# An attention, expert and FFN kernel: first expert chosen from two batches, five attention buffers, rows in sorted order

## The chip, the cores and the metric

One core of one Trainium2 chip runs the whole kernel. The metric is device time in microseconds (us) of one execution. The engines are named as in the profile: PE (TensorE matmul), PEld (its weight loads), DVE (VectorE), ACT (ScalarE), POOL (GpSimd) and SP (SyncE, which here only issues transfers).

## The reference

Three stages follow each other. Shapes: batch 4, 8 heads, 768 positions, head size 64, so 3072 tokens of 512 numbers.

```python
# 1. chunked attention: 24 chunks of 32 queries, each with 16 positions to the left,
#    8 to the right, and 8 memory keys
scores = scale * q_c @ k_full.T; a = softmax(scores); out[:, :, c] = a @ v_full
# 2. top-1 mixture of 8 experts on x = (tokens, 512)
logits = xn @ en.T / tau                 # xn, en: rows divided by their norms
expert_idx = argmax(logits); gate_w = softmax(logits)[expert_idx]
out[mask_e] = gate_w * (relu(x[mask_e] @ w1[e]) @ w2[e])      # w1 512x1024, w2 1024x512
# 3. FFN
h = x @ w_in; g = relu(h) ** 2; y = g @ w_out                 # 512 -> 2048 -> 512
```

## The kernel before, in words

**Attention** runs over 32 iterations i (4 batches, 4 pairs of heads, 2 halves of the sequence), as a software pipeline over the engines with five more iterations to empty it. In iteration i PE does, in this order, `sp` (scores of i, L277, 24 matmuls in two groups of 12), `op` (values of i-2, L336), `lp` (router products, L382), `tp` (transposes of the weights of i-1, L324) and `xp` (transposes of the output of i-3, L371). DVE does a small `memset` into `sp`, `rs` (row sums, L311), in every second iteration the inverse of the sums (L317, L318), `mx` (L293), `e` (scores minus maxima, L301) and `xa` (output scaled, L350). ACT copies `tp` to `pt`, takes exponents of `e`, copies `xp` to `xt` and takes squares of rows for the norms. POOL lays the windows of keys into `kw` for iteration i+2 (two copies L135 and one of the memory keys L267). SP loads q, k and v (`qt`, `kt`, `vb`, 384 KB each and v twice that per pair of iterations). Before the change q, k and v have three buffers each.

When the four pairs of heads of a half batch are through, `dp` and a copy give its `dots` (the router logits, 3 tiles of 128 tokens), and the rows go to `x_d` in DRAM.

**Early choice.** The generator `early` is stepped between the parts of the last attention iterations. It counts over finished tiles which expert is most frequent (`cs`, `cm`, `sel`, `ks`, then the number `e_i`, which SP and POOL read as a register in order to start loading the weights of that expert, `r1a`, `r1b`), ranks the tokens of that expert over 18 of the 24 tiles (three batches; `m0`, `p0`, `g0`, `osl`, `lf`, then a comparison with a row of numbers into `scratch`, `rid`, `ip`, `iv`), and gathers 2 slots of 128 of its rows from `x_d`. So the first expert can start before the routing of all the rest is known. The weights are split into a high and a low part in fp32r: a cast on ACT (`wh1a`, `wh1b`) and a subtraction on DVE (`wl1a`, `wl1b`); the split of `r1a` is step W0, that of `r1b` W1. Steps are listed in a string, by the (iteration minus 32) in which they stand: x0, x1 transpose the gathered rows, A0 begins the first product (`hps`).

**Routing.** After the last `dots`, `stp` (PE, counts per expert) starts a chain of small DVE operations (`ce`, `key`, `ahead`, `tri_c`, `byp`, `pm`, `dlr`, `pos`, `osl`, `rid`, `ohl`), which gives each token its slot (31 slots of 128). The experts of the other slots and then the FFN follow; from there on PE is nearly always busy.

Of the kernel before, what the change touches and what calls it, by code (L numbers as in the profile page):

```python
# [9 lines left out]
F32 = mybir.dt.float32  # L10
# [11 lines left out]
def kernel(  # L22
# [70 lines left out]
    ks = route.tile([P, 1], F32, name="ks")  # L93
    e0 = route.tile([P, 1], F32, name="e0")
# [5 lines left out]
    sumb = route.tile([P, 2, 2, E], BF16, name="sumb")  # L100
# [118 lines left out]
    def attention(actx, hooks, space, drain):  # L219
# [6 lines left out]
        q_p = qk_ctx.enter_context(tc.tile_pool(name="qt", bufs=3))  # L226
# [5 lines left out]
        NV, NW, NK_, LAG = 3, 3, 3, 2  # L232
# [189 lines left out]
        nc.scalar.copy(out=vb[1][:, 0].rearrange("p c d -> p (c d)"), in_=kt[0][:, 0:1].to_broadcast([P, 2 * NC * D]))  # L422
# [6 lines left out]
        clear_kw(0, nc.vector)  # L429
        clear_v(1, 1, nc.vector)  # L430
# [5 lines left out]
        clear_kw(1, nc.vector)  # L436
        windows(1)
        def start_en():
# [3 lines left out]
            vec.extend([lambda: next(gen, None)] * 17)  # L442
# [6 lines left out]
        def finish_en():  # L449
# [7 lines left out]
            0: [lambda: clear_v(2, 0, nc.gpsimd), start_en, lambda: clear_kw(2, nc.vector)],  # L457
            1: [lambda: clear_v(2, 1, nc.gpsimd)],
# [3 lines left out]
        load_q(1)  # L462
        load_k(2)
# [18 lines left out]
        for i in range(NK + LAG + 3):  # L482
            if i == NK:
                qk_ctx.close()
                space()
# [82 lines left out]
    def tally(c, pool, part):  # L568
# [3 lines left out]
        lt = pool.tile([P, E, n], F32, name=f"lt{part}", tag=f"lt{part}")  # L572
        sums = pool.tile([P, 2, E, 1], F32, name=f"sums{part}")
        revb = c["rev"].unsqueeze(1).to_broadcast([P, n, E])
        kmb = km[:, T0:T1].to_broadcast([P, n, E])
        nc.vector.tensor_tensor(out=o, in0=revb, in1=kmb, op=ALU.is_equal)
        yield
        nc.vector.tensor_tensor(out=lt.rearrange("p e t -> p t e"), in0=kmb, in1=revb, op=ALU.is_gt)
        yield
        nc.vector.tensor_reduce(out=sums[:, 1], in_=o.rearrange("p t e -> p e t"), op=ALU.add, axis=AX.X)  # L580
        yield
        nc.vector.tensor_reduce(out=sums[:, 0], in_=lt, op=ALU.add, axis=AX.X)
        yield
        nc.vector.tensor_copy(out=sumb[:, part], in_=sums.rearrange("p j e o -> p j (e o)"))
        yield

    def early(c, per, ps, begin, gather):
# [9 lines left out]
        G = 2 * HT  # L597
        kme = km[:, 0:TE].rearrange("p t o -> p (t o)")
        pe = p0g[:, 0:TE].rearrange("p t o -> p (t o)")
        nc.vector.memset(p0g[:, TE:NT], 0.0)  # L600
        o0 = t([P, TE, E], BF16, "o0")
        for T0 in range(0, TE, G):
# [6 lines left out]
            yield int(T0 + G < TE)  # L609
        yield from gap((6, 1, 6, 1, 8, 6)[0])  # L610
        cp = ps.tile([P, G, E], F32, name="cp", tag="a")
        for T0 in range(0, TE, G):
            nc.tensor.matmul(out=cp, lhsT=c["ones"], rhs=o0[:, T0:T0 + G], start=T0 == 0, stop=T0 + G == TE)
        yield from gap((6, 1, 6, 1, 8, 6)[1])
# [11 lines left out]
        yield  # L626
        m0 = t([P, TE], BF16, "m0")
        nc.vector.tensor_scalar(out=m0, in0=kme, scalar1=ks, scalar2=None, op0=ALU.is_equal)
        nc.vector.tensor_scalar(out=e_i, in0=ks, scalar1=-1.0, scalar2=float(E), op0=ALU.mult, op1=ALU.add)
        begin()  # L630
        nc.vector.tensor_scalar(out=e0, in0=ks, scalar1=-1.0, scalar2=float(E), op0=ALU.mult, op1=ALU.add)
        yield from gap((6, 1, 6, 1, 8, 6)[2])
        p0 = ps.tile([P, TE], F32, name="p0", tag="a")
        nc.tensor.matmul(out=p0, lhsT=c["upper"], rhs=m0, start=True, stop=False)
        for T in range(TE - 1):
            nc.tensor.matmul(
                out=p0[:, T + 1:TE], lhsT=c["ones"], rhs=m0[:, T:T + 1].to_broadcast([P, TE - 1 - T]),
                start=False, stop=T == TE - 2,
            )
        yield from gap((6, 1, 6, 1, 8, 6)[3])  # L640
        g0 = t([P, TE], F32, "g0")
        nc.vector.scalar_tensor_tensor(
            out=g0, in0=p0, scalar=float(KE * P), in1=m0, op0=ALU.is_lt, op1=ALU.mult
        )
        yield
        nc.vector.tensor_tensor(out=pe, in0=p0, in1=g0, op=ALU.mult)
        yield
        osl = t([P, TE, KE], F32, "osl")
        nc.vector.scalar_tensor_tensor(
            out=osl[:, :, 1], in0=pe, scalar=float(P), in1=g0, op0=ALU.is_ge, op1=ALU.mult  # L650
        )
        yield
        lf = t([P, TE], BF16, "lf")
        nc.vector.scalar_tensor_tensor(
            out=lf, in0=osl[:, :, 1], scalar=-float(P), in1=pe, op0=ALU.mult, op1=ALU.add
        )
        nc.vector.tensor_tensor(out=osl[:, :, 0], in0=g0, in1=osl[:, :, 1], op=ALU.subtract)
        yield
        rid = t([P, TE, 2, KE], BF16, "rid")
        ohs = [c["scratch"].bitcast(BF16)[:, T * P:(T + 1) * P] for T in range(TE)]  # L660
        all_ohs = c["scratch"].bitcast(BF16).rearrange("p (t x) -> p t x", x=P)
        for T in range(0, TE, G):
            nc.vector.tensor_tensor(
                out=all_ohs[:, T:T + G], in0=c["iota_b"].unsqueeze(1).to_broadcast([P, G, P]),
                in1=lf[:, T:T + G].unsqueeze(2).to_broadcast([P, G, P]), op=ALU.is_equal,
            )
            yield
            yield
        nc.vector.tensor_tensor(
            out=rid[:, :, 0, :], in0=osl,  # L670
            in1=c["iota"][:, 0:TE].unsqueeze(2).to_broadcast([P, TE, KE]), op=ALU.mult,
        )
        yield
        nc.vector.tensor_scalar(out=rid[:, :, 1, :], in0=osl, scalar1=c["p1"], scalar2=None, op0=ALU.mult)
        yield from gap((6, 1, 6, 1, 8, 6)[4])
        ip = ps.tile([P, 2, KE], F32, name="ip", tag="a")
        for T in range(TE):
            nc.tensor.matmul(out=ip, lhsT=ohs[T], rhs=rid[:, T], start=T == 0, stop=T == TE - 1)
        iv = t([P, KE], F32, "iv")
        nc.vector.tensor_scalar(out=iv, in0=ip[:, 0, :], scalar1=float(P), scalar2=-1.0, op0=ALU.mult, op1=ALU.add)  # L680
        yield
        nc.vector.tensor_tensor(out=iv, in0=iv, in1=ip[:, 1, :], op=ALU.add)
        yield
        nc.vector.tensor_scalar(out=gid[:, 0:KE], in0=iv, scalar1=0.0, scalar2=None, op0=ALU.max)
        gather()
        yield from gap((6, 1, 6, 1, 8, 6)[5])
# [3 lines left out]
        yield  # L690
        for _ in tally(c, per, 0):
            yield

    def routing(rp, c):
# [48 lines left out]
        stp = ps_r[1].tile([P, 2, E], F32, name="stp", tag="t")  # L743
# [15 lines left out]
        for part in range(2):  # L759
# [888 lines left out]
```

## Time and the profile before

| what | value |
|---|---|
| median of 3 runs (range) | 1003.68 us (1002.71 to 1005.19) |
| profiled execution: its own time / span | 1003.92 us / 1002.3 us |
| PE busy, share of span | 954.9 us, 95% |
| PE weight loads | 825.6 us, 82% |
| DVE / ACT / POOL busy | 620.3 / 386.7 / 163.1 us |
| DMA moved, mean rate | 216.91 MB, 216 GB/s |

The profiled execution is one of the same kernel; its span is what the trace covers, and 1.6 us of its time lie around the span. Busy time is summed over the whole span; a wait counts only if nothing else fills it.

### The profile page before, as it was taken

How to read it: one execution, taken by the hardware profiler on the slowest of the kernel's cores; microseconds unless marked ns; L12 is line 12 of the kernel's file. 1: busy time of each engine (PE TensorE's matmuls, PEld its weight loads, DVE VectorE, ACT ScalarE, POOL GpSimd, SP SyncE). 2: the span in 40 equal slices, each digit the busy share in tenths (PEclk: the TensorE clock that was granted, in tenths of full speed). 3: DMA queues.
4: the chain of work that ended last, by engine and by line, in shares of the span. 5: the costliest groups of instructions: out<-in, count | busy, mean ns of one | idle time of the engine just before them, and what ended most of it. 6: DMA issues, size and time to landing. Idle time of an engine off the chain costs nothing.

```text
span 1002.3 us, 19228 instructions
## 1 busy us (share of the span) xinstructions
PE 954.9 (95%) x6992; PEld 825.6 (82%) x6992; DVE 620.3 (62%) x1166; ACT 386.7 (39%) x690; POOL 163.1 (16%) x193
## 2 busy tenths in 40 slices
PE   5898698999999999999899999999999999999997
PEld 3776577888887887887899989989989989999996
DVE  7888896556856777886687653643554453455332
ACT  3566632545545555666434222311221211132111
POOL 7665311111211121220000010010001001001001
PEclk8999999999999999999999999999999999999999
DMA  7889626554857577895896584574556557545621
GB/s 270 285 313 335 202 87 221 171 178 130 294 199 275 205 255 251 311 354 190 299 340 211 169 272 147 177 267 166 173 192 234 174 195 238 196 156 182 223 78 43
DMA packets 75751, 216.91 MB, mean 216 GB/s; under 512 B 8433, under 2 KB 8561, under 8 KB 75648
## 3 DMA queue, kind: packets, MB, share of 16 engines
q1 hardware_dynamic: 55488, 166.30, 48.3%
q10 hardware_dynamic: 12768, 25.70, 7.3%
q0 software_dynamic: 7392, 23.60, 6.7%
q8 instruction: 57, 0.93, 0.4%
q14 instruction: 46, 0.38, 0.1%
HBM read 257.51 MB, written 38.80 MB: 296 GB/s over the span
## 4 chain that ended last, share of the span: by engine, by line
issue 65%; DMA 16%; POOL 2%; POOLq 0%
DMA y_d<-ysb,sidx 16%; POOL out_dram L1347 2%; POOLq L1644 0%; POOLq L1018 0%; POOLq L1347 0%; POOLq L1144 0%; POOLq L1590 0%
## 5 line engine op out<-in xcount | busy, mean ns | idle before, releaser
L1327 PE MATMUL acc<-wo,g 128*128 128x512 f32 x384 | 150.0, 391 | 0.0
L1326 PE MATMUL acc<-wo,g 128*128 128x512 f32 x384 | 149.8, 390 | 0.0
L1325 PE MATMUL acc<-wo,g 128*128 128x512 f32 x384 | 149.6, 390 | 0.0
L1347 POOL DMA_INDIRECT out_dram<-osb,oid x24 | 26.2, 1090 | 485.9 <-ACT osb L1343 475.8
L1384 DVE TENSOR_TENSOR cf<-zY,v 128x512 f32<-128x512 f32 x24 | 16.6, 691 | 137.6 <-PE zY L1300 137.6
L108 DVE TENSOR_TENSOR g<-cf,g 128x1024 fp32r<-128x1024 f32 x48 | 58.8, 1225 | 60.6 <-ACT g L105 60.6
L105 ACT CAST g<-cf 128x1024 fp32r<-128x1024 f32 x48 | 50.6, 1055 | 118.1 <-DVE cf L1385 68.4
L1381 ACT COPY cf<-zX 128x512 f32<-128x512 f32 x24 | 14.1, 585 | 201.3 <-PE zX L1300 201.3
L1327 PEld LDWEIGHTS acc<-wo,g 128*128 128x128 f32 x384 | 72.1, 188 | 15.1
L1325 PEld LDWEIGHTS acc<-wo,g 128*128 128x128 f32 x384 | 72.3, 188 | 13.4
L1326 PEld LDWEIGHTS acc<-wo,g 128*128 128x128 f32 x384 | 72.1, 188 | 13.4
L1300 PEld LDWEIGHTS zX<-yc,ww 128*128 128x128 f32 x576 | 74.6, 189 | 3.5
L1144 POOL DMA_INDIRECT y_d<-ysb,sidx x28 | 32.6, 1163 | 273.4 <-ACT ysb L1143 222.9
L1300 PE MATMUL zY<-yc,ww 128*128 128x256 f32 x576 | 76.9, 283 | 0.0
L1300 PE MATMUL zW<-yc,ww 128*128 128x256 f32 x576 | 76.9, 283 | 0.0
L1300 PE MATMUL zX<-yc,ww 128*128 128x256 f32 x576 | 76.6, 282 | 0.0
L1300 PEld LDWEIGHTS zY<-yc,ww 128*128 128x128 f32 x576 | 72.6, 192 | 0.1
L1300 PEld LDWEIGHTS zW<-yc,ww 128*128 128x128 f32 x576 | 72.6, 192 | 0.0
L135 POOL COPY kw<-kt 64x672 f32<-64x672 f32 x62 | 50.9, 821 | 33.6 <-PE sp L277 20.3
L1095 PE MATMUL yps<-wh2a,hTha 128*128 128x512 f32 x112 | 46.2, 412 | 0.3 <-ACT ysb L1143 0.3
L108 DVE TENSOR_TENSOR hTlb<-tr,hThb 128x512 fp32r<-128x512 f32 x28 | 19.3, 690 | 42.9 <-ACT hThb L105 42.6
L1095 PE MATMUL hps<-wh1b,xT 128*128 128x512 f32 x104 | 42.5, 409 | 1.8 <-ACT ha L1112 1.8
(315 smaller groups left out, 2055.4 us busy)
## 6 DMA issues: line engine op xcount, KB each, us to landing
ww<-wi_d SPq DMA_DIRECT2D x161, 512.0 KB
r1a<-in_moe_w_dram SPq DMA_DIRECT2D x54, 512.0 KB
r1b<-in_moe_w_dram SPq DMA_DIRECT2D x54, 512.0 KB
r2a<-in_moe_w_dram SPq DMA_DIRECT2D x52, 512.0 KB
r2b<-in_moe_w_dram SPq DMA_DIRECT2D x52, 512.0 KB
wi_d<-ww SPq DMA_DIRECT2D x28, 512.0 KB
vb<-in_v_dram SPq DMA_DIRECT2D x32, 384.0 KB
rw<-in_moe_w_in_dram ACTq DMA_DIRECT2D x32, 256.0 KB
```

The costliest lines, as they stand in the source:

```text
L105: nc.scalar.copy(out=hi, in_=src)
L108: eng.tensor_tensor(out=lo, in0=src, in1=hi.bitcast(F32), op=ALU.subtract)
L135: (nc.vector if eng == "v" else nc.gpsimd).tensor_copy(out=out, in_=in_)
L1095: nc.tensor.matmul(out=out_ps, lhsT=ah, rhs=wh, start=first, stop=False)
L1144: nc.gpsimd.indirect_dma_start(out=y_d[:, :], out_offset=bass.IndirectOffsetOnAxis(ap=sidx[:, s:s + 1], axis=0), in_=y, in_offset=None, bo ...
L1300: nc.tensor.matmul(out=z[:, jj, :], lhsT=w[:, wx, kt, c], rhs=y[:, yx, kt, :], start=start and (jj, kt, x) == (0, 0, 0), stop=(jj, kt, x) ...
L1325: nc.tensor.matmul(out=self.acc[j], lhsT=a, rhs=wh, start=s0, stop=False)
L1326: nc.tensor.matmul(out=self.acc[j], lhsT=a, rhs=wl, start=False, stop=False)
L1327: nc.tensor.matmul(out=self.acc[j], lhsT=b_, rhs=wh, start=False, stop=s1)
L1347: ins = nc.gpsimd.indirect_dma_start(out=out[:, :], out_offset=bass.IndirectOffsetOnAxis(ap=oid[:, jj:jj + 1], axis=0), in_=o, in_offset=N ...
L1381: nc.scalar.copy(out=c1[:, 0], in_=z)
L1384: nc.vector.tensor_tensor(out=c1[:, 1], in0=z, in1=v, op=add)
```

## The change

1. **Buffers and the start.** q, k and v get five buffers. The loads of v run three pairs ahead (one before), those of k five (three before), those of q four (two before). The buffers `kw1`, `kw2` and `vb1` to `vb4` are cleared by ACT copies of a zero column and no longer by DVE and POOL (one half of `vb1` stays on DVE); the clears of `vb` are spread over the ends of iterations 0 to 6. Of the 17 tiny steps that give the norms of the expert embeddings, 6 run at once, and the others are put one by one between the steps of iterations 0 to 3, where they all ran before iteration 2. All stores of x to `x_d` go out on POOL's queue (those of batches 0 to 2 were on ACT's).
2. **First expert from two batches.** It is counted over 12 tiles at iterations 20 and 21 (over 18 tiles at 28 and 29 before). The ranks of these 12 tiles follow at once, those of the next 6 tiles at iteration 28 and 29. The register reads and the loads of `r1a` and `r1b` stand ahead of iteration 25, the gathers on POOL ahead of the windows of iteration 31.
3. **Weights split inside attention.** W0 stands at the end of iteration 30 and W1 at the end of iteration 31 (before: 32 and 34); x0, x1 at 32 and A0 at 33 (before: 33 and 34).
4. **Sorted order.** The positions in the sorted list are worked out with counts of whole tokens and not of slots: `tally` loses a comparison and a reduction, `stp` is 8 wide instead of 16, and PE loses two matmuls over all 24 tiles. After `stp` there are an ACT copy, wider operations (`tri` 128, `begins` 16, `pm` and `dlr` over 384 and 48), and small new ones (`lack`, two for `byp`, one for `sd2`).

```diff
-        q_p = qk_ctx.enter_context(tc.tile_pool(name="qt", bufs=3))
+        q_p = qk_ctx.enter_context(tc.tile_pool(name="qt", bufs=5))
...
-        NV, NW, NK_, LAG = 3, 3, 3, 2
+        NV, NW, NK_, LAG = 5, 3, 5, 2
...
-                (nc.gpsimd if b == B - 1 else nc.scalar).dma_start(out=x_d[T0 * P:(T0 + HT) * P, :].rearrange("(t p) d -> p t d", p=P), in_=xa)
+                nc.gpsimd.dma_start(out=x_d[T0 * P:(T0 + HT) * P, :].rearrange("(t p) d -> p t d", p=P), in_=xa)
...
+            if eng is nc.scalar:
+                n, w = t.shape[0], t.shape[1] * t.shape[2]
+                eng.copy(out=t.rearrange("p a b -> p (a b)"), in_=kt[0][0:P, 0:1][P - n:P].to_broadcast([n, w]))
...
-        clear_kw(1, nc.vector)
-        windows(1)
...
-            vec.extend([lambda: next(gen, None)] * 17)
+            for _ in range(6):
+                next(gen, None)
+            vec.extend([lambda: next(gen, None)] * 11)
...
+        later = {
+            0: [lambda: clear_v(1, 0, nc.scalar), lambda: load_v(1)],
+            1: [lambda: clear_v(2, 0, nc.scalar)],
+            2: [lambda: clear_v(2, 1, nc.scalar), lambda: load_v(2)],
...
+            if i == NK - 7:
+                cst["rooms"]()
...
-            while vec and i > 0:
+            while vec and i > 2:
...
-                for f, n in ((load_v, 1), (load_k, 3), (load_q, 2)):
-                    if i // 2 + n < NK // 2:
+                for f, n in ((load_v, 3), (load_k, 5), (load_q, 4)):
+                    if i // 2 + n < NK // 2 and (f is not load_v or i > 5):
...
+        yield from ranks(0, TC, 6)
+        yield 1
+        for _ in choose(c, per, TC, TE):
+            pass
+        yield from ranks(TC, TE, 0)
...
-            c = attention(actx, hooks, space, lambda n: run({(0, -1): 'W0', (1, -1): 'x0 x1 q', (2, -1): 'A0 p q W1 q', (3, -1): 'p q p q', (4, -1): 'N q q q p'}.get(n, "")))
+            c = attention(actx, hooks, space, lambda n: run({(-2, -1): 'W0', (-1, -1): 'W1', (0, -1): 'q x0 x1 q', (1, -1): 'q A0 p q', (2, -1): 'p p q', (3, -1): 'p p q', (4, -1): 'N q'}.get(n, "")))
```

On DVE, at the start of the program, this stands between the setup of the memory keys (`mkT`) and the first exponents (`e`) before:

```order
L434 COPY mkT_141<-scratch_140 64x128 x2
L402 MEMSET kw1_135 64x768 x2
L402 MEMSET kw2_136 64x768 x2
L286 MEMSET sp_192 32x32
L116 TENSOR_SCALAR ena_206<-ensq_144 8x1
L117 TENSOR_SCALAR ens_207<-ena_206 8x1
L293 TENSOR_REDUCE mx_211<-sp_192 128x6
L119 TENSOR_SCALAR ens_207<-ens_207 8x1
L301 TENSOR_TENSOR e_214<-sp_192,mx_211 128x384
```

and this of the change, from the same place (`ens`, `ent` and `ena` are the tiny steps):

```order
L442 COPY mkT_146<-scratch_145 64x128 x2
L117 TENSOR_SCALAR ena_191<-ensq_149 8x1
L118 TENSOR_SCALAR ens_192<-ena_191 8x1
L120 TENSOR_SCALAR ens_192<-ens_192 8x1
L123 RECIPROCAL ent_193<-ens_192 8x1
L125 SCALAR_TENSOR_TENSOR ent_193<-ent_193,ena_191 8x1
L127 SCALAR_TENSOR_TENSOR ens_192<-ens_192,ent_193 8x1
L123 RECIPROCAL ent_193<-ens_192 8x1
L287 MEMSET sp_215 32x32
L125 SCALAR_TENSOR_TENSOR ent_193<-ent_193,ena_191 8x1
L294 TENSOR_REDUCE mx_230<-sp_215 128x6
L127 SCALAR_TENSOR_TENSOR ens_192<-ens_192,ent_193 8x1
```

The four clears of `kw1` and `kw2` have left DVE, and six tiny steps have come ahead of its first work on `sp`.

On PE, the scores of iteration 29 (`sp_2017`) stand in the change behind the matmuls of the ranks (`p0`, which read `m0` of DVE):

```order
L664 MATMUL p0_1993<-e_m0_1528,ones_b_643 128x2
L664 LDWEIGHTS ones_b_643
L664 MATMUL p0_1993<-e_m0_1528,ones_b_643 128x1
L278 MATMUL sp_2017<-kw2_139,q_1438 32x128 x12
L337 MATMUL op_2032<-vb3_143,pt_1974 32x128 x12
L383 MATMUL lp_2046<-xt_1982,enT_147 32x128 x3
L700 LDWEIGHTS scratch_145
L700 MATMUL ip_2060<-e_rid_1532,scratch_145 128x4
```

where before the matmuls of the ranks came later, behind `op` and `lp` of iteration 30 (`sp_1994`):

```order
L277 MATMUL sp_1994<-kw0_134,q_1768 32x128 x12
L336 MATMUL op_2008<-vb2_139,pt_1942 32x128 x12
L382 MATMUL lp_1860<-xt_1960,enT_142 32x128 x3
L634 LDWEIGHTS upper_b_625
L634 MATMUL p0_2027<-e_m0_1963,upper_b_625 128x18
L636 LDWEIGHTS ones_b_620
```

So `sp` of iteration 29 now stands directly behind a step that needs the choice of the last finished tiles.

On DVE, the end of attention before (`xa_1817` is the output of iteration 31, `spare` are the gathered rows):

```order
L108 TENSOR_TENSOR wl1a0_2153<-r1a0_100,wh1a0_2152 128x1024
L108 TENSOR_TENSOR wl1a1_2155<-r1a1_101,wh1a1_2154 128x1024
L350 TENSOR_TENSOR xa_1817<-op_2245,rs_2110 128x3x128
L108 TENSOR_TENSOR spare0_2159<-tr_2269,spare0_2159 128x512
L108 TENSOR_TENSOR spare1_2160<-tr_2276,spare1_2160 128x512
L108 TENSOR_TENSOR wl1b0_2185<-r1b0_102,wh1b0_2184 128x1024
L108 TENSOR_TENSOR wl1b1_2187<-r1b1_103,wh1b1_2186 128x1024
L135 COPY dots_78<-dp_2314 128x24
```

and of the change:

```order
L109 TENSOR_TENSOR wl1a0_1718<-r1a0_101,wh1a0_1717 128x1024
L109 TENSOR_TENSOR wl1a1_1720<-r1a1_102,wh1a1_1719 128x1024
L289 MEMSET sp_2187 32x16
L312 TENSOR_REDUCE rs_2217<-e_2165 128x6
L294 TENSOR_REDUCE mx_2219<-sp_2187 128x6
L302 TENSOR_TENSOR e_2221<-sp_2187,mx_2219 128x384
L351 TENSOR_TENSOR xa_1916<-op_2201,rs_2051 128x3x128
L109 TENSOR_TENSOR wl1b0_1752<-r1b0_103,wh1b0_1751 128x1024
L109 TENSOR_TENSOR wl1b1_1754<-r1b1_104,wh1b1_1753 128x1024
L312 TENSOR_REDUCE rs_2217<-e_2221 128x6
```

Both pairs of subtractions now stand ahead of work of iterations that are still to come, the first ahead of the maxima of iteration 31.

## Rows read from the trace of the kernel before

**Rows 1.** Windows of the span: busy us of each engine, clock, DMA.

```profile
0.00:100.00 100.00, 79.79 (x1729) 63.37 (x1729) 82.61 (x241) 53.96 (x128) 66.03 (x104) 0.97 0.86 300
...
200.00:300.00 100.00, 100.00 (x492) 83.21 (x492) 65.31 (x131) 49.99 (x91) 19.83 (x17) 1.00 0.59 199
```

**Rows 2.** Timeline of PE, 5 to 128 us: start, duration, instruction, idle before it.

```profile
8.23 1.47 PE L277 MATMUL sp<-kw,q 128*32 128x128 f32 x24 [0.30 <-POOL kw L267]
...
19.75 1.51 PE L336 MATMUL op<-vb,pt 128*32 128x128 f32 x24 [3.25 <-DVE sp L288]
...
23.19 0.86 PE L277 MATMUL sp<-kw,q 128*32 128x128 f32 x24
...
58.55 0.86 PE L277 MATMUL sp<-kw,q 128*32 128x128 f32 x24
...
64.03 0.86 PE L277 MATMUL sp<-kw,q 128*32 128x128 f32 x24
...
70.07 0.86 PE L277 MATMUL sp<-kw,q 128*32 128x128 f32 x24
...
94.45 0.86 PE L277 MATMUL sp<-kw,q 128*32 128x128 f32 x24
...
102.45 0.56 PE L636 MATMUL p<-e_m,ones_b 128*128 128x17 bf16 x17
...
127.18 0.17 PE L760 MATMUL stp<-sumb,ones_b 128*128 128x16 bf16 x1 [0.73 <-DVE sumb L584]
```

**Rows 3.** Timeline of DVE, the start.

```profile
6.11 0.70 DVE L402 MEMSET kw<- 64x768 f32 x1 [0.22 <-issue]
...
9.58 0.09 DVE L286 MEMSET sp<- 32x32 f32 x1
...
13.24 0.29 DVE L124 SCALAR_TENSOR_TENSOR ent<-ent,ena 8x1 f32<-8x1 f32 x1
...
17.14 0.09 DVE L286 MEMSET sp<- 32x32 f32 x1
```

**Rows 4.** Timeline of DVE, one pair of iterations of the ring.

```profile
59.51 0.09 DVE L286 MEMSET sp<- 32x32 f32 x1 [0.71 <-PE sp L277]
```

**Rows 5.** Waits of PE between 30 and 95 us: total, times, longest.

```profile
PE sp L277 <- DMA q<-in_q_dram: 1.6, 2, 1.1
```

**Rows 6.** Timeline of DVE, from the early choice to the routing.

```profile
100.64 0.20 DVE L616 TENSOR_REDUCE e_cs<-cp 128x8 f32<-128x48 f32 x1
...
105.14 0.94 DVE L663 TENSOR_TENSOR scratch<-iota_b,e_lf 128x768 bf16<-128x768 bf16 x1
...
115.51 2.36 DVE L108 TENSOR_TENSOR wl1a<-r1a,wh1a 128x1024 fp32r<-128x1024 f32 x2 [1.36 <-ACT wh1a L105]
117.79 0.55 DVE L350 TENSOR_TENSOR xa<-op,rs 128x384 f32<-128x384 f32 x1
...
129.38 0.36 DVE L792 TENSOR_TENSOR pm<-oh,byp 128x192 f32<-128x192 bf16 x1
```

**Rows 7.** Timeline of ACT: a clear, a copy of `tp`, and the cast of W0.

```profile
2.17 1.47 ACT L422 COPY vb<-kt 128x1536 f32<-128x1536 f32 x1
...
60.85 0.48 ACT L133 COPY pt<-tp 128x384 f32<-128x384 f32 x1 [1.25 <-PE tp L324]
...
114.43 1.99 ACT L105 CAST wh1a<-r1a 128x1024 fp32r<-128x1024 f32 x2
```

**Rows 8.** Timeline of POOL: windows of keys, and a store of rows of x.

```profile
61.97 1.68 POOL L135 COPY kw<-kt 64x672 f32<-64x672 f32 x2 [0.38 <-PE sp L277]
...
114.45 0.81 POOL L368 DMA_DIRECT2D x_d<-xa  x1 [0.94 <-DVE xa L350]
```

**Rows 9.** Windows: iteration 28 to `stp`, a stretch of lower clock, the routing.

```profile
94.45:127.18 32.73, 23.75 (x408) 18.00 (x408) 26.55 (x83) 20.05 (x47) 8.65 (x11) 0.95 0.68 231
...
112.00:114.00 2.00, 1.97 (x16) 1.18 (x8) 1.91 (x9) 0.48 (x1) 1.21 (x2) 0.50 0.50 127
...
127.00:162.00 35.00, 30.52 (x184) 24.10 (x184) 31.04 (x88) 10.37 (x18) 3.36 (x3) 1.00 0.37 125
```

More of the change, by code (lines that the diff above doesn't have):

```diff
@@ L493, in attention @@
                 drain((i - NK, order.index((f, lag))))
-            while vec and i > 0:
+            while vec and i > 2:
                 vec.pop(0)()
+            for f in later.get(i, []):
+                f()
             if i == starts[0] - 1:
@@ L600, in early @@
         nc.vector.memset(p0g[:, TE:NT], 0.0)
-        o0 = t([P, TE, E], BF16, "o0")
-        for T0 in range(0, TE, G):
+        o0 = t([P, TC, E], BF16, "o0")
+        for T0 in range(0, TC, G):
             for _ in choose(c, per, T0, T0 + G):
@@ L608, in early @@
             )
-            yield int(T0 + G < TE)
-        yield from gap((6, 1, 6, 1, 8, 6)[0])
+            yield int(T0 + G < TC)
+        yield from gap(6)
         cp = ps.tile([P, G, E], F32, name="cp", tag="a")
-        for T0 in range(0, TE, G):
-            nc.tensor.matmul(out=cp, lhsT=c["ones"], rhs=o0[:, T0:T0 + G], start=T0 == 0, stop=T0 + G == TE)
-        yield from gap((6, 1, 6, 1, 8, 6)[1])
+        for T0 in range(0, TC, G):
+            nc.tensor.matmul(out=cp, lhsT=c["ones"], rhs=o0[:, T0:T0 + G], start=T0 == 0, stop=T0 + G == TC)
+        yield
         cs = t([P, E, 1], F32, "cs")
@@ L630, in early @@
[L630 to L639, printed above, removed]
@@ L652, in early, with ranks @@
-        yield
         lf = t([P, TE], BF16, "lf")
[L654 to L658, printed above, removed]
         rid = t([P, TE, 2, KE], BF16, "rid")
-        ohs = [c["scratch"].bitcast(BF16)[:, T * P:(T + 1) * P] for T in range(TE)]
         all_ohs = c["scratch"].bitcast(BF16).rearrange("p (t x) -> p t x", x=P)
[L662 to L665, printed above, removed]
+        def ranks(Ta, Tb, wait):
+            n = Tb - Ta
+            nc.vector.tensor_scalar(out=m0[:, Ta:Tb], in0=kme[:, Ta:Tb], scalar1=ks, scalar2=None, op0=ALU.is_equal)
+            yield from gap(wait)
+            p0 = ps.tile([P, n], F32, name="p0", tag="a")
+            nc.tensor.matmul(out=p0, lhsT=c["upper"], rhs=m0[:, Ta:Tb], start=True, stop=False)
+            for T in range(Tb - 1):
+                T1 = max(T + 1, Ta)
+                nc.tensor.matmul(
+                    out=p0[:, T1 - Ta:n], lhsT=c["ones"], rhs=m0[:, T:T + 1].to_broadcast([P, Tb - T1]),
+                    start=False, stop=T == Tb - 2,
+                )
+            yield
+            g, q, o, f, r = g0[:, Ta:Tb], pe[:, Ta:Tb], osl[:, Ta:Tb], lf[:, Ta:Tb], rid[:, Ta:Tb]
+            nc.vector.scalar_tensor_tensor(
+                out=g, in0=p0, scalar=float(KE * P), in1=m0[:, Ta:Tb], op0=ALU.is_lt, op1=ALU.mult
@@ new lines, in ranks @@
+            yield
+            nc.vector.scalar_tensor_tensor(out=f, in0=o[:, :, 1], scalar=-float(P), in1=q, op0=ALU.mult, op1=ALU.add)
+            nc.vector.tensor_tensor(out=o[:, :, 0], in0=g, in1=o[:, :, 1], op=ALU.subtract)
+            yield
+            for T in range(Ta, Tb, G):
+                nc.vector.tensor_tensor(
+                    out=all_ohs[:, T:T + G], in0=c["iota_b"].unsqueeze(1).to_broadcast([P, G, P]),
+                    in1=lf[:, T:T + G].unsqueeze(2).to_broadcast([P, G, P]), op=ALU.is_equal,
+                )
+                yield
@@ L690, in early @@
         yield
+        mp = ps.tile([P, 1], F32, name="mp", tag="a")
+        nc.tensor.matmul(out=mp, lhsT=c["ones"], rhs=mb, start=True, stop=True)
         for _ in tally(c, per, 0):
             yield
+        lack = c["lack"] = per.tile([P, 1], F32, name="e_lack")
+        nc.vector.tensor_scalar(out=lack, in0=mp, scalar1=-1.0, scalar2=float(KE * P), op0=ALU.mult, op1=ALU.add)
+        nc.vector.tensor_scalar(out=lack, in0=lack, scalar1=0.0, scalar2=None, op0=ALU.max)
+        yield
+        nc.vector.tensor_copy(out=lackr, in_=lack)
+        yield
     def routing(rp, c):
```

172 lines of the change are left out of this document (93 added, 79 removed).

## The prediction, made before the change was run

> **What bounds the kernel now.** I read the windows first, then the timeline of PE through attention, then what DVE does in the gaps. PE is busy 79.79 of the first 100 us and 100.00 of the third [rows 1]. From about 170 us on the kernel is a stream that PE paces, so the change, whose parts all lie before that, can gain or lose only what it does to the moment at which the stream begins; everything behind shifts as a whole.
>
> In attention the pace is a ring: `sp` on PE, `mx` and `e` on DVE, the exponent on ACT, and back. Two iterations take 64.03 - 58.55 = 5.48 us [rows 2], and DVE is idle .71 us of them, while it waits for `sp` [rows 4]. So DVE is nearly full: more than .71 us of extra DVE work per pair makes the ring longer. Two waits of `sp` for q cost 1.6 us together [rows 5]. Behind the ring comes the start of the routing, `stp` at 127.18 [rows 2], and then a stretch in which DVE is busy 31.04 of 35 us [rows 9]: DVE paces there too.
>
> The places that are not at the ring's pace are the start (iteration 4 begins at 23.19, where four iterations at 2.74 us would need 11 us) and the end of attention (iteration 28 at 94.45, `stp` 32.73 us later). These are where the change acts. The sum has four terms, for the stretches up to iteration 4, up to 28, up to `stp`, and behind it.
>
> **Start, up to iteration 4.** Before, DVE clears `kw1` and `kw2` (four times .70, with .2 between, from 6.11 on) and only then does its first `memset` into `sp`, at 9.58 [rows 3]. PE was through with `sp` of iteration 0 before 8.23, when it began that of iteration 1 [rows 2]. Later DVE does nothing but tiny steps from 13.24 to 17.14 [rows 3], and PE waits 3.25 us for that at 19.75 [rows 2]. The change takes both away: six tiny steps, about 1.3 us, stand ahead of the first `memset`, which I put at 8.05 (-1.5), and the solid block of 3.9 us is spread over the idle places of iterations 0 to 3. Those add up to 5.4. What comes in are clears on ACT, 1.47 each [rows 7]: the one after the first exponent delays `pt` by about 1 us, which hardly matters while `op` waits for it only at iteration 2. Step by step I get iteration 4 at about 17.8 in place of 23.19: **-5.4**. Bounds: -5.5 (all of it) and -3.5 (the clears on ACT and the spread steps take 2 back).
>
> **Iterations 4 to 20** stay 70.07 - 23.19 = 46.88 us [rows 2]. The clears of `vb3` and `vb4` (1.47 each) are to fit in the 1.25 us that ACT is idle ahead of `pt` [rows 7]; the .2 by which each is too long lies ahead of the copy of `xt`, for which nobody waits so soon. A clear that delayed `pt` each time would cost 4 x .2 = .8. Stores of x on POOL cost it .81 each [rows 8], one in four iterations. Its windows take 2 x (1.68 + .34) of the 5.48 us of a pair [rows 8], so it has about 1.4 free.
>
> **Iterations 20 to 28.** Counting, which stood at 28 and 29, comes here: eight small operations of about .2 [rows 6]. The ranks of 12 tiles add seven more of that size and two comparisons of .94 [rows 6]: 1.6 + 1.4 + 1.9 = 4.9 us on DVE. Four pairs of iterations give 4 x .71 = 2.8 us of slack. Eight iterations at the pace of 4 to 20 take 46.88 / 2 = 23.4; this stretch took 94.45 - 70.07 = 24.4, because of the waits for q, which go if q is loaded four ahead. So 23.4 + 4.9 - 2.8 = 25.5, and half a us more since not all slack lies where the work stands: 26.0, **+1.6**. Bounds: +0.5 (most of it hidden) and +3.9 (no slack usable).
>
> **Iteration 28 to `stp`.** Less DVE work: about 1.9 of comparisons and 1.6 of counting have gone, and `lt` and its reduction. But three waits come in.
> - `sp` of iteration 29 stands behind the ranks' matmuls, which wait for the choice from the `dots` of iteration 28. `dots`, four operations and `m0` take 1.5 us on DVE, then come .56 us of small matmuls [rows 2], .86 of `sp`, and the `memset` that waits for it. Nothing else lies ready on DVE, since `memset` is ahead of the ranks in its queue: iteration 29 starts 2.4 us later. I take it whole.
> - W0 stands at the end of iteration 30: ACT can cast only after the exponent and the copy of `xt`, each about as long as the .48 of `pt` [rows 7]. The cast of both halves is 1.99 [rows 7], so the first half is ready 1.5 us after DVE had nothing more to do; then DVE subtracts for 2.36 [rows 6] ahead of the `memset` of iteration 31. W1 does the same one iteration later. Before, W0's subtraction waited 1.36 too [rows 6], but behind it stood only one `xa` of attention. So 2 x (1.5 + 2.36) = 7.7 us now lie in the ring, and what is late next is `op` of iteration 29 and the last `xa`.
> - In exchange the stretch from the last `xa` to `stp` loses W1 (2.36 and its wait): 8.8 us become about 6.5, as `dp` still stands behind six matmuls of A0.
>
> Laid out in a row from 94.45, the last `xa` ends 29.0 us later in place of 23.9 (118.34, [rows 6]), and `stp` 35.5 later in place of 32.7: +2.8. PE has idle stretches of 3.8 and 4.8 us in it. Before, a busy share of about a half ahead of 112 was followed by a window at a granted clock of .50, the 1.2 GHz level [rows 9], where a group of `sp` takes 1.47 in place of .86 [rows 2]. I add .7 for the part of this that falls on the path: **+3.5**. Bounds: the DVE work alone (26.55 of the 32.73 us, less 4.7, plus .9, with the idle time of before, 6.2) gives 29, which is -3.7; and a path at the low clock all the way gives +7.
>
> **Behind `stp`.** `pm` takes .36 over 192 elements [rows 6]; over 384 I take .65, `dlr` the same, so +.6; three small operations for `byp` and `sd2` are +.5, and the rest cancels: **+1.0**, on a stretch that DVE paces. Bounds 0 and +1.1.
>
> **Sum.** -5.4 + 1.6 + 3.5 + 1.0 = +0.7. The profiled execution took 1003.92 against a span of 1002.3 (1.6 around it), .24 over the median of 1003.68. So 1003.7 + .7 = **1004.4**. About 0.3%, 3 us, is what can be told from no change here: the forecast is no change.
>
> **The stores of x.** [rows 8] show one store on POOL issued in .81 us, next to busy DVE. The Trainium skill ("SBUF — State Buffer", section "SBUF: two separate sides") warns that a DMA issued from GpSimd's queue is held up while DVE runs one of its two-port operations, since GpSimd then can't write the descriptors, and advises ACT's or SP's queue. By the trace six more such stores cost nothing; by the rule each would be held for one DVE operation. That is the fourth rival below.
>
> **Rivals.**
> 1. *The end is not stretched* (faster). DVE has less to do from 28 to `stp`, and if casts and the ranks' wait hide behind it, the stretch is 29 us and not 35.5 to 36.2. Sum -5.4 + 1.6 - 3.7 + 1.0 = -6.5: **997**. For it: the DVE work itself [rows 9]. Against: the order of the queues. Chance .22.
> 2. *The clock* (slower). PE goes through the idle stretches of iterations 29 to 33, falls to the 1.2 GHz level, as at 112 to 114 [rows 9], and stays there until `stp`: `op`, `lp`, `xp` and the first products of A0 at 1.47/.86 = 1.7 times their time. About 6 us of PE work on the path become 10: +4.2 more, of which .7 is in the sum: **1008**. It decides from the point at which A0 begins at the low level. The skill ("TensorE: Matmul & The Clock Gate", section "HAM oscillation — how this bites in real kernels") describes idle gaps that send PE back to the low level again and again; by that, both idle stretches would cost, as in this rival. Chance .16.
> 3. *The early start is swallowed* (the change does not do what it says). v of pair 1 is loaded only after ACT has cleared its half of `vb1`; I have it land at 17 to 18, needed at 18.5. Every us later is a us lost, up to 5.4; half of it gives **1007**. Before, PE waited for no v in attention, for the loads were first in the queue. Chance .12.
> 4. *POOL's queue.* A store that is held for one `e` (.56) pushes the windows beyond POOL's 1.4 us of slack: with six stores +2 to 3, **1007**. Chance .04.
>
> The forecast has .46, of which some two thirds lie within 3 us, the rest split evenly. Faster: .22 and .08 = .30. Slower: .08 and most of the rivals 2, 3 and 4: .27. Same: .43. The range runs from 997.5, near the first rival, to 1009.5, above the second: some 2 in 10 are outside. The forecast's own range is 1001 to 1007.
>
> **What would show it.** The start of iteration 4 in PE's timeline (17.8), the first `memset` on DVE (8.05), the length of iterations 20 to 28 (26.0), PE's wait of `sp` 29 for DVE `m0`, DVE's idle ahead of `wl1a` and `wl1b` (1.5 each, now in iterations 30 and 31), `stp` at about 17.8 + 46.9 + 26.0 + 36.2 = 126.9, and the granted clock from 110 to 125. A wait of `op` for a DMA of `vb` ahead of 20 us would speak for rival 3, `stp` before 122 for rival 1. I would be wrong above all if the waits of iterations 29 to 31 overlap with each other.

## The result, and the profile after

The changed kernel is slower: 1009.76 us median of 20 runs against 1004.14 of 20 runs of the kernel before, ratio 1.0052 with a 95% interval of 1.0038 to 1.0067, some 5 us. The forecast was no change, 1004.4 against 1003.7; on that scale the ratio gives 1008.9. The profiled execution has a span of 1008.0 us where it was 1002.3, +5.7.

The timeline of PE gives the stations that the prediction named (start, duration, instruction, idle before it):

```profile
17.58 0.86 PE L278 MATMUL sp<-kw,q 128*32 128x128 f32 x24
18.96 0.86 PE L337 MATMUL op<-vb,pt 128*32 128x128 f32 x24 [0.52 <-DMA vb<-in_v_dram]
...
58.02 0.71 PE L337 MATMUL op<-vb,pt 128*32 128x128 f32 x17 [0.45 <-issue]
...
66.33 0.86 PE L278 MATMUL sp<-kw,q 128*32 128x128 f32 x24
...
70.01 0.82 PE L337 MATMUL op<-vb,pt 128*32 128x128 f32 x18
72.37 0.31 PE L337 MATMUL op<-vb,pt 128*32 128x128 f32 x3 [1.54 <-issue]
...
80.91 0.86 PE L337 MATMUL op<-vb,pt 128*32 128x128 f32 x24 [3.26 <-DVE xa L351]
...
95.67 0.86 PE L278 MATMUL sp<-kw,q 128*32 128x128 f32 x24
...
100.47 0.17 PE L661 MATMUL p<-e_m,upper_b 128*128 128x6 bf16 x1 [1.72 <-DVE e_m L658]
...
111.46 0.86 PE L278 MATMUL sp<-kw,q 128*32 128x128 f32 x24 [2.37 <-POOL kw L268]
...
117.51 1.51 PE L337 MATMUL op<-vb,pt 128*32 128x128 f32 x24 [3.51 <-ACT e L306]
...
132.99 0.17 PE L795 MATMUL stp<-sumb,ones_b 128*128 128x8 bf16 x1 [1.77 <-DVE sumb L601]
```

Iterations 4, 20 and 28 begin at 17.58, 66.33 and 95.67, `stp` at 132.99. Beside [rows 2]:

| stretch | before | after | difference | predicted |
|---|---|---|---|---|
| start to iteration 4 | 23.19 | 17.58 | -5.6 | -5.4 |
| iterations 4 to 20 | 46.88 | 48.75 | +1.9 | 0 |
| iterations 20 to 28 | 24.38 | 29.34 | +5.0 | +1.6 |
| iteration 28 to `stp` | 32.73 | 37.32 | +4.6 | +3.5 |
| `stp` to the end of the span | 875.1 | 875.0 | -0.1 | +1.0 |
| sum | 1002.3 | 1008.0 | +5.7 | +0.7 |

The start went as forecast and was lost twice over. The losses can be read off the same rows. A group of `op` breaks off at 70.83 and goes on only at 72.37, 1.54 us later, with no instruction to blame. The `op` at 80.91 has waited 3.26 us for `xa`. In the end there is a wait of 1.72 for the choice and one of 3.51 in which DVE subtracts, both forecast, and one of 2.37 for the windows behind the gathers, which was not. At that place, `sp` of iteration 31, the kernel before has a wait for the windows too, so only .9 of it is new:

```profile
105.24 0.86 PE L277 MATMUL sp<-kw,q 128*32 128x128 f32 x24 [1.51 <-POOL kw L267]
```

DVE's timeline in the changed kernel shows what it did meanwhile, and answers to [rows 3, 6]:

```profile
8.13 0.09 DVE L287 MEMSET sp<- 32x32 f32 x1 [0.20 <-PE sp L278]
...
77.89 0.65 DVE L676 SCALAR_TENSOR_TENSOR e_osl<-p0g,e_g 128x12 f32<-128x12 f32 x1
78.58 0.17 DVE L678 SCALAR_TENSOR_TENSOR e_lf<-e_osl,p0g 128x12 bf16<-128x12 f32 x1
...
79.35 0.95 DVE L682 TENSOR_TENSOR scratch<-iota_b,e_lf 128x768 bf16<-128x768 bf16 x1
80.22 0.55 DVE L351 TENSOR_TENSOR xa<-op,rs 128x384 f32<-128x384 f32 x1
...
102.33 0.17 DVE L676 SCALAR_TENSOR_TENSOR e_osl<-p0g,e_g 128x6 f32<-128x6 f32 x1
...
112.93 2.36 DVE L109 TENSOR_TENSOR wl1a<-r1a,wh1a 128x1024 fp32r<-128x1024 f32 x2 [1.44 <-ACT wh1a L106]
...
118.84 2.36 DVE L109 TENSOR_TENSOR wl1b<-r1b,wh1b 128x1024 fp32r<-128x1024 f32 x2 [1.44 <-ACT wh1b L106]
...
135.32 0.56 DVE L828 TENSOR_TENSOR pm<-oh,begins 128x384 f32<-128x384 bf16 x1
```

The first `memset` came at 8.13 (forecast 8.05), the waits for the casts are 1.44 each (1.5). Windows of three stretches, with columns as in [rows 1] (clock and DMA share are the third and second numbers from the end):

```profile
40.00:70.00 30.00, 26.45 (x574) 20.47 (x575) 23.48 (x68) 17.90 (x47) 21.91 (x34) 1.00 1.03 414
113.00:117.00 4.00, 1.00 (x12) 0.64 (x6) 3.91 (x7) 1.86 (x5) 0.00 (x0) 0.95 0.00 0
117.00:127.00 10.00, 8.76 (x86) 6.78 (x86) 5.95 (x10) 6.07 (x12) 2.52 (x4) 0.51 0.24 89
```

From 113 to 117 us PE works 1.00 of 4 us, and from 117 to 127 it runs at a granted clock of .51, the 1.2 GHz level: `op` takes 1.51 there.

### The profile page after: what moved, and what is told of

It reads as the page before. It is cut to its first block, busy times and chain, and to the rows that moved or that the text cites. A ratio compares the mean times of both kernels' runs of the same rounds, so it can differ in the third digit from the quotient of the medians.

```text
span 1008.0 us, 19273 instructions
## 1 busy us (share of the span) xinstructions
PE 959.9 (95%) x7002; PEld 829.2 (82%) x7002; DVE 620.3 (62%) x1177; ACT 398.0 (39%) x701; POOL 165.4 (16%) x197
## 4 chain that ended last, share of the span: by engine, by line
issue 65%; DMA 15%; POOL 2%; POOLq 0%
DMA y_d<-ysb,sidx 15%; POOL out_dram L1390 2%; POOLq L1689 0%; POOLq L1061 0%; POOLq L1390 0%; POOLq L1187 0%; POOLq L1635 0%
## 5 line engine op out<-in xcount | busy, mean ns | idle before, releaser
L337 PE MATMUL op<-vb,pt 128*32 128x128 f32 x768 | 31.0, 288 | 15.7 <-ACT e L306 5.0
```

Of the source, the lines that this page charges most:

```text
L337: nc.tensor.matmul(out=op[32 * j:32 * j + 32, c // 4], lhsT=pt[:, c // 4, 32 * j:32 * j + 32], rhs=vt[:, :, c0 + c, :], start=True, stop=True,
```

## Experiments

Twelve variants were run. Each was timed against the kernel before on the same chip; the stretches are those of the table above, from each run's own trace.

| run | ratio (95%) | iteration 4 | 4 to 20 | 20 to 28 | 28 to `stp` | `stp` |
|---|---|---|---|---|---|---|
| kernel before | 1 | 23.19 | 46.88 | 24.38 | 32.73 | 127.18 |
| changed kernel | 1.0052 (1.0038 to 1.0067) | 17.58 | 48.75 | 29.34 | 37.32 | 132.99 |
| 1 start alone | .9949 (.9934 to .9964) | 18.55 | 47.78 | 24.36 | 33.01 | 123.70 |
| 2 split back | 1.0054 (1.0036 to 1.0072) | 18.62 | 47.65 | 30.34 | 34.36 | 130.97 |
| 3 ranks spread | 1.0035 (1.0021 to 1.0049) | 17.56 | 47.64 | 27.46 | 38.91 | 131.57 |
| 4 loads nearer | 1.0049 (1.0031 to 1.0067) | 18.15 | 49.23 | 29.44 | 36.41 | 133.23 |
| 5 start alone, stores on ACT | .9950 (.9933 to .9967) | 18.55 | 46.98 | 23.42 | 32.96 | 121.91 |
| 6 start and sorted order | .9962 (.9947 to .9977) | 17.57 | 47.58 | 24.35 | 33.18 | 122.68 |
| 7 last ranks later | 1.0042 (1.0023 to 1.0061) | 18.02 | 48.42 | 29.73 | 36.17 | 132.34 |
| 8 = 2 + 3 + 7 | 1.0019 (1.0001 to 1.0037) | 18.70 | 47.94 | 26.90 | 35.73 | 129.27 |
| 9 stores on ACT | 1.0029 (1.0013 to 1.0045) | 18.19 | 46.97 | 28.29 | 37.04 | 130.49 |
| 10 = 8, gathers behind | .9996 (.9976 to 1.0016) | 17.94 | 48.23 | 26.88 | 31.32 | 124.37 |
| 11 = 10, stores on ACT | .9971 (.9952 to .9990) | 19.01 | 47.57 | 26.57 | 33.00 | 126.15 |
| 12 gathers behind alone | 1.0066 (1.0043 to 1.0090) | 17.56 | 48.40 | 29.68 | 34.94 | 130.58 |

One thing must be known to read it. Each execution lists its mean granted clock, and executions of one kernel differ in it: .982 to .997 over 7 runs of the last kernel in the table, from 1010.95 us down to 1004.78. Over all 222 executions here, lines of one common slope through each kernel's own runs fall by .46 us per .001 of clock, which accounts for about a third of the spread. So stretches of a single trace, above all the one from 28 to `stp`, can carry a us or two of that, and where ratio and stretch disagree the ratio decides. By the widths of the intervals, two of these ratios differ beyond noise only from .002 to .003 on, which is 2 to 3 us.

**1. The start alone.** Parts 2 to 4 of the change are left out.

```diff
+        NV, NW, NK_, LAG = 5, 3, 5, 2
...
+            for _ in range(6):
+                next(gen, None)
+            vec.extend([lambda: next(gen, None)] * 11)
...
```

> Part 1 of the change alone (five buffers, clears on ACT, the spread start, loads further ahead, all stores of x on POOL), the expert choice, the split and the order as before. By the step sum iteration 4 begins 5.6 us earlier as in the changed kernel. If the 1.9 us that iterations 4 to 20 lost there came from the loads further ahead, they are lost here too: -3.7 us, about 1000. If they came with the rest of the change, -5.6, about 998. If a stretch later gives the start back, no difference from before.

It is 5.1 us faster than the kernel before; of the -4.6 at iteration 4 in its trace .9 was lost up to 20 and .3 from there to `stp`. That lies between the -3.7 and the -5.6 of the expectation: a part of the 1.9 us that iterations 4 to 20 lost is lost here too. Part 1 is a gain by itself, and parts 2 to 4 cost some 10 us.

**2. The split back.**

```diff
-{(-2, -1): 'W0', (-1, -1): 'W1', (0, -1): 'q x0 x1 q', (1, -1): 'q A0 p q', (2, -1): 'p p q', (3, -1): 'p p q', (4, -1): 'N q'}
+{(0, -1): 'W0', (1, -1): 'x0 x1 q', (2, -1): 'A0 p q W1 q', (3, -1): 'p q p q', (4, -1): 'N q q q p'}
...
-run("N2 N3 a1 c0 b0 ...
+run("N2 p9 N3 a1 c0 b0 ...
```

The second string lists the steps behind attention; the step p9 there returns with the old places.

> The changed kernel with W0, x0, x1, A0 and W1 where they stood before the change. Theory A (the split inside the ring costs the end): iteration 28 to stp takes some 33 to 34 us and not 37.3, so 3 to 4 us less than the changed kernel, about +1.5 to +2 against before. Rival (the end is bound by the ranks' wait and the windows behind the gathers): 36 us or more, at most 1 us better than the changed kernel.

In its trace the end is 3.0 us shorter, as theory A said, but the ratio did not move, as the rival said. One trace against 6 runs: the split inside the ring is not shown to cost anything by itself. Its trace had a clock of 1.00 from 100 to 135 us, the changed kernel's had .83, so part of the 3.0 is likely clock.

**3. The ranks spread.** Ten steps between the operations instead of one, from the third on.

```diff
-        yield from ranks(0, TC, 6)
+        yield from ranks(0, TC, 6, 9)
```

> The changed kernel with the ranks of the 12 tiles one operation per iteration (10 steps between them, same instructions, from iteration 21 to 25) and not in one block. Theory A (the block stands ahead of xa, so the slack of the other pairs goes unused): PE's wait of 3.3 us for xa goes and iterations 20 to 28 take about 26 to 27 us in place of 29.3, so 2.5 to 3 us less than the changed kernel. Rival (the DVE work itself, or instruction fetch behind full DMA queues, sets the length): 28.5 or more.

Iterations 20 to 28 took 27.46, 1.9 less, and the ratio fell by .0017, which by itself is within the noise. The timeline of PE shows that no `op` of these iterations waits for `xa` any more:

```profile
75.39 0.86 PE L278 MATMUL sp<-kw,q 128*32 128x128 f32 x24
77.06 0.86 PE L337 MATMUL op<-vb,pt 128*32 128x128 f32 x24 [0.80 <-DVE sp L289]
...
83.17 0.86 PE L337 MATMUL op<-vb,pt 128*32 128x128 f32 x24 [0.98 <-DVE sp L289]
```

The same instructions cost less when each meets a pair's own slack. Theory A, a little under its size.

**4. Loads nearer.**

```diff
-            6: [lambda: clear_v(4, 1, nc.scalar), lambda: load_v(4), lambda: load_v(5)],
+            6: [lambda: clear_v(4, 1, nc.scalar), lambda: load_v(4)],
...
-                for f, n in ((load_v, 3), (load_k, 5), (load_q, 4)):
-                    if i // 2 + n < NK // 2 and (f is not load_v or i > 5):
+                for f, n, m in ((load_v, 1, 5), (load_k, 3, 5), (load_q, 2, 4)):
+                    if m <= i // 2 + n < NK // 2:
```

> The changed kernel, five buffers and the same start, but in the steady part v is loaded one pair ahead, k three and q two, as before the change. Theory A (loads far ahead fill the DMA queues, 1.03 of their time from 40 to 70 us, and PE's instruction stream then comes late: idle gaps inside a group of matmuls that no instruction explains, 2.5 us, and stretched groups): iterations 4 to 20 take 46.9 and not 48.7, the gaps inside groups go, 2 to 3.5 us less in all. Rival (gaps have another cause): 48 or more and the gaps stay; waits for q come back as before, up to +1.6.

Theory A fell: 49.23 from 4 to 20, and the waits of PE between 30 and 95 us still hold the gaps (total, times, longest); a wait for q has come, at 30.48:

```profile
PE op L337 <- issue: 2.0, 3, 1.3
PE sp L278 <- DMA q<-in_q_dram: 1.2, 1, 1.2
```

Without the wait for q the stretch would be 48.0, the rival's bound. How far ahead the loads run is not what causes the gaps. The DMA share from 40 to 70 us was 1.03 here as well, so whether full queues matter was not decided by this.

**5 and 9. Stores on ACT**, in the start alone and in the changed kernel.

```diff
-                nc.gpsimd.dma_start(out=x_d[T0 * P:(T0 + HT) * P, :]...
+                (nc.gpsimd if b == B - 1 else nc.scalar).dma_start(out=x_d[T0 * P:(T0 + HT) * P, :]...
```

> Part 1 of the change as in the run of the start alone, but the stores of x of batches 0 to 2 stay on ACT's queue. Theory (the 2.1 us of gaps inside groups of op that no instruction explains, 0.2, 0.6 and 1.3 at 58, 64 and 72 us, come from stores on POOL): the gaps go and iterations 4 to 20 take 47 us, so 1 to 2 us under the start alone, about 998. Rival (the gaps belong to the earlier start itself, PE's instruction stream comes at its own pace): gaps stay, within 1 us of the start alone.

> The changed kernel with the stores of x of batches 0 to 2 back on ACT's queue, nothing else. Theory A (stores on POOL make PE's instruction stream late, as the start alone with and without them showed: 1.8 us up to stp): no gaps inside op, iterations 4 to 20 in 47.0, 20 to 28 in about 28, stp 1.5 to 2.5 us earlier than in the changed kernel. Rival (in the changed kernel the gaps lie beside DVE work that sets the pace anyway): gaps go, stp moves by less than 1 us.

The gaps go in both. PE's timeline around iteration 20, first with the stores on POOL (start alone):

```profile
70.02 0.82 PE L336 MATMUL op<-vb,pt 128*32 128x128 f32 x18
72.10 0.31 PE L336 MATMUL op<-vb,pt 128*32 128x128 f32 x3 [1.27 <-issue]
```

and then on ACT (the same kernel otherwise):

```profile
68.54 0.86 PE L277 MATMUL sp<-kw,q 128*32 128x128 f32 x24
69.22 0.84 PE L336 MATMUL op<-vb,pt 128*32 128x128 f32 x24
```

The window from 40 to 70 us of the latter has a DMA share of .90 in place of 1.03:

```profile
40.00:70.00 30.00, 27.28 (x629) 21.77 (x618) 24.86 (x73) 19.57 (x51) 19.68 (x31) 1.00 0.90 331
```

A gap of 1.2 to 1.5 us at 71 to 73 us stands in all ten traces with the stores on POOL and in none of the three with them on ACT, nor in the kernel before (run 11 has one of .52 at 58.9). Iterations 4 to 20 take 46.98 and 46.97 in runs 5 and 9, the 46.88 of before. In time the repair is worth 2.3 us in the changed kernel (1.0029 against 1.0052; the intervals overlap, and the difference is just beyond its noise), and nothing is to be told of it in the start alone (.9950 against .9949), where the trace had `stp` 1.8 us earlier.

**6. Start and sorted order**, so the change without parts 2 and 3. The edit is part 1 and part 4 of the diff, with the three operations for `lack` put into the early choice of before.

> Parts 1 and 4 of the change (start and sorted order); expert choice, ranks and split as before, so the changed kernel without parts 2 and 3. By the prediction's fourth term +1.0 against the start alone, about 1000.7; by the trace of the changed kernel, in which the time behind stp is the same as before (875.0 and 875.1), +0: 999.7. Either way parts 2 and 3 would then cost 8 to 10 us, by the difference from the changed kernel.

.9962 against .9949 of run 1: +1.3 us, with intervals that overlap. Neither 0 nor the +1.0 of the prediction is excluded. What is clear is the difference to the changed kernel: parts 2 and 3 cost 9.0 us, give or take 2.

**7. Last ranks later.**

```diff
-        yield from ranks(TC, TE, 0)
+        yield from ranks(TC, TE, 6)
```

> The changed kernel with the matmuls of the last six tiles' ranks six steps later, behind sp, op and lp of iteration 29 and not ahead of sp. Theory A (sp of iteration 29 waits 1.7 us for the choice and DVE then 1.5 for sp): iteration 28 to 29 takes 3.0 us in place of 5.3 and stp comes 1.5 to 2.5 us earlier. Rival (the wait only moves, to ip and the casts behind it): 28 to stp stays at 36.5 to 37.5 us.

Iteration 28 to 29 took 3.0 us, as theory A said, but 28 to `stp` gave back only 1.1 of the 2.3. PE's timeline shows where the wait went:

```profile
99.18 0.86 PE L278 MATMUL sp<-kw,q 128*32 128x128 f32 x24
...
104.24 0.29 PE L700 MATMUL ip<-e_rid,scratch 128*128 128x4 bf16 x6 [2.01 <-DVE e_rid L690]
```

In the changed kernel the same `ip` waited 1.21:

```profile
104.31 0.29 PE L700 MATMUL ip<-e_rid,scratch 128*128 128x4 bf16 x6 [1.21 <-DVE e_rid L690]
```

So .8 of it moved to `ip`, as the rival said, and more to what follows: `sp` of iteration 31 stood 15.55 us behind that of 28, beside 15.79 in the changed kernel. The ratio fell by .0010, less than can be told.

**8, 10, 11. Repairs together.** Run 8 has the edits of 2, 3 and 7. Run 10 also puts the gathers on POOL behind the windows, run 11 the stores on ACT:

```diff
-        gather()
+        c["pend"] = gather
...
                 windows(i + 2)
+            cst.pop("pend", lambda: None)()
```

> The changed kernel with three things together: ranks of 12 tiles spread, last ranks six steps later, W0 to W1 at their places before the change. If the three causes are separate and add up (1.9 for the block, 3.0 for the split, 2 for the wait): about 7 us under the changed kernel, 1002 to 1003. If they hide each other: at most 4 us under it, 1005 or more.

> As the run with three things together (ranks spread, last ranks later, split back), and the two gathers on POOL behind the windows of iteration 31 and not ahead. Theory A (sp of iteration 31 waited 2.4 us for windows that stood behind the gathers): that wait goes, 28 to stp takes about 33.5 in place of 35.7, 2 us less in all. Rival (x0 and A0 then wait for gathered rows instead): at most .5 us.

> The changed kernel with all five repairs: ranks spread, last ranks later, split back, gathers behind, stores on ACT. If the early choice itself is then paid only by its 4.9 us of DVE work, of which the ring has 2.8 free: stp at 125.5 to 126.5, 1002 to 1003, some 1.5 us under the kernel before and still 4 above the start alone with stores on ACT. Rival (nothing left to pay): 998 to 999, as the start alone.

Run 8 is 3.3 us under the changed kernel, not 7. The 7 were added up from stretches of single traces. By the ratios the three repairs alone gave -.2, 1.7 and 1.0 us, 2.5 in all, so these times do not show that they hide each other; it is in the traces that a wait moved on (run 7 above, run 12 below). Run 10 takes up another wait. POOL's timeline in run 8, with the gathers ahead of the windows of iteration 31:

```profile
104.19 1.03 POOL L1061 DMA_INDIRECT mx<-x_d,gid  x1 [0.30 <-issue]
105.23 0.79 POOL L136 COPY kw<-kt 64x672 f32<-64x672 f32 x1
107.86 0.79 POOL L136 COPY kw<-kt 64x672 f32<-64x672 f32 x1 [1.84 <-DMA mx<-x_d,gid]
```

Here the windows are done at 109, and `sp` of iteration 31 starts at 109.11; in run 10 it starts at 104.36:

```profile
101.73 0.86 PE L278 MATMUL sp<-kw,q 128*32 128x128 f32 x24
...
104.36 0.86 PE L278 MATMUL sp<-kw,q 128*32 128x128 f32 x24
...
124.37 0.17 PE L796 MATMUL stp<-sumb,ones_b 128*128 128x8 bf16 x1 [0.97 <-DVE sumb L602]
```

That is another 2.3 us by the ratios, theory A's 2 but within the noise of the two; in the traces, where run 10 had a mean clock of .998 and run 8 one of .992, it is 4.4. With all five repairs the kernel is 2.9 us faster than before, and by the ratios 2.1 behind the start alone with the stores on ACT, again within the noise: between theory and rival, nearer to the theory. The traces show a rest in iterations 20 to 28: 26.57 us against 23.42, 3.1 us for the 4.9 us of DVE work that the prediction counted.

**12. The gathers behind alone**, in the changed kernel.

> The changed kernel with only the two gathers on POOL moved behind the windows of iteration 31. Theory A (in the changed kernel DVE's subtraction of W0 stands ahead of the work on sp of iteration 31, until 115.3, so the 2.4 us that sp waits for the windows lie beside it): sp of iteration 31 comes 2 us earlier, 28 to stp shrinks by less than 1 us. Rival (the wait is on the path here too): 28 to stp 35 in place of 37.3, 2 us less in all.

`sp` of iteration 31 came at 108.43 instead of 111.46, and then `op` waited in its place:

```profile
108.43 0.86 PE L278 MATMUL sp<-kw,q 128*32 128x128 f32 x24
...
116.87 1.51 PE L337 MATMUL op<-vb,pt 128*32 128x128 f32 x24 [3.98 <-ACT e L306]
```

The time did not fall (1.0066; by the two intervals a gain of more than 1.5 us is excluded). The 2.4 us shorter end of its trace goes with an execution at a clock of .997, the fastest of its seven: from 117 to 127 us its granted clock was .85, where the changed kernel's was .51. Theory A: the wait for the windows lay beside W0's subtraction. In run 10, where the split stands elsewhere, the same step came with 2.3 us less; that it pays only there is likely and, with this noise, not shown.

## Why the prediction was off, step by step

On the prediction's scale the changed kernel takes 1008.9 us: inside the stated range of 997.5 to 1009.5, outside the forecast's own 1001 to 1007. It is close to the price of rival 2 (1008), but that is luck in the main: rival 2 put its 4.2 us into the end of attention, and of the 5 us that the sum missed about 1 lies there; the rest lies in iterations 4 to 28.

- **Start, -5.4**: right. -5.6 in the trace, the first `memset` and iteration 4 within .3 us, and run 1 ends 5.1 us faster. Over the thirteen traces with this start iteration 4 began between 17.56 and 19.01. The sign of rival 3 came, but small: `op` waited .52 us for v, at 18.96, and .54 in run 12; in the other eleven traces it did not wait for v.
- **Iterations 4 to 20, 0**: the step that failed is "Stores of x on POOL cost it .81 each". I asked only whether POOL had room. POOL had, for PE waited for no windows there; PE lost. Of the 1.9 us, .52 are the wait for v and .45 the gap before 58.02; the rest are groups that were drawn out. With the stores on ACT the stretch is 46.97. In the start alone, without a wait for v, the stores made .8 of difference.
- **Iterations 20 to 28, +1.6**: this is the term that was mis-sized most, +5.0. The step that failed is "4 x .71 = 2.8 us of slack", with only half a us taken off. The ranks stood in one block ahead of `xa` at 80.22, in one pair of iterations, whose slack is .71; the others' went unused. With the stores on ACT (run 9) the stretch was 28.29, which is +3.9: the bound that I gave for no slack usable (its clock there was .94, so a little of this may be clock). Spreading the ranks gave 1.9 back, stores on ACT 1.0. With both (run 11) the stretch was 26.57, beside a forecast of 26.0. The DVE work itself was well sized: DVE was busy 4.6 us more in this stretch in run 9 than in run 5, beside my 4.9. One of the small operations was longer than the .2 I took, `osl` with .65 at 77.89; POOL copied windows then, but the next one took .17 beside the same copies, so the cause is open.
- **Iteration 28 to `stp`, +3.5**: right in its waits (1.72, 1.44, 1.44) and a little small, +4.6. The clock lay at .51 from 117 to 127 us, more than I had allowed for with .7 us. That is rival 2 in part: over the runs, the changed kernel has a mean clock of .9900 and the kernel before .9927, which by the .46 us per .001 makes some 1.2 of the 5 us, an estimate. The page "TensorE: Matmul & The Clock Gate" of the Trainium skill (section "HAM oscillation — how this bites in real kernels") tells of idle gaps that send PE back to the low clock. This trace agrees: PE was busy 1.00 of the 4 us up to 117, and its clock then fell to .51. I had not seen that `sp` 31 would wait for the gathers on POOL, 2.37 in place of 1.51; run 12 shows no gain from taking that away as long as the split stood there.
- **Behind `stp`, +1.0**: `pm` took .56 and not .65. The span behind `stp` did not grow in the trace, and run 6 leaves 0 to +1 open.
- **Rival 4** had the right part of the change and the wrong way. The Trainium skill ("SBUF — State Buffer", section "SBUF: two separate sides") warns of stores on GpSimd's queue; its remedy, ACT's queue, is what helped. But the reason that it gives, a DMA that is held up and leaves the DMA engines idle, was not seen: the stores issued in .76 to .95 us each, the DMA share from 40 to 70 us was 1.03, and the lost time is idle PE inside a group. From issue to landing the stores took 10.6 us (median of eight), beside 4.2 for the two on POOL in the kernel before; what part of that is the full DMA was not told apart.

Of the 9.0 us of parts 2 and 3 that run 6 leaves, the four repairs that concern them (run 10) take back 5.6; the stores, which belong to part 1, give 2.5 more (run 11). One by one the five repairs gave 3.4 us in all by the ratios, together 8.1; the noise of five differences leaves open how much of that they give only in company. What stays open besides: why PE's stream breaks off with the stores on POOL (a fuller DMA and the queue itself were not told apart), and how much of the end is the split and how much is clock.

## What to carry to other kernels

Slack of a ring is to be had once per turn: count work against the slack of the turn in which it stands, not against the sum over turns, and spread it. When several waits stand in a row, removing one shows the next, as in runs 7 and 12; undoing a whole part (here the start alone) tells what a part is worth. The fastest versions here are that part by itself, with the stores on POOL's queue or on ACT's: .9949 and .9950 of the kernel before, not to be told apart, and 10 us under the changed kernel.

## What the runs showed of the hardware

- PE broke off inside a group of 24 matmuls without a wait on any engine, for 1.54 us at 70.8 (1.17 to 1.27 in the nine other traces with the stores on POOL). The DMA view of the changed kernel shows a packet of the instruction queue q8 between 69.8 and 70.0 us and the next one from 73.6 (the columns are packets, MB and their share of 16 engines in that window):

```profile
q8 instruction: 1, 0.02, 32.8%
```

  The packet before it is at 61.8. In all ten traces with the gap this distance is 7.6 to 8.0 us, and PE goes on 2.3 to 2.6 us behind the second packet (read in windows of .2 us); in runs 5, 9 and 11, which have no gap, the same two packets lie 5.6 to 6.2 us apart. So with the stores on POOL an instruction packet comes some 2 us late, just ahead of the gap. That PE waits for its instructions there is the likeliest reading; that q8 is PE's queue, and why the packet is late, is not shown.
- One program's executions differ in mean granted clock by up to .015, and time goes with it, .46 us per .001. That accounts for about a third of the spread among executions of one kernel (87 of the kernel before lie between 999.66 and 1010.53 us); what makes the rest is open.
